# Attention rows of three query blocks turned by the PE instead of a transposing DMA, with three more decode pieces in the lead-in

## The chip, the cores and the metric

The kernel runs on one core of one Trainium2 chip. The metric is the device time of one execution in microseconds (us); the times given for the kernel before are a median of three runs. The engines are PE (TensorE, matmuls), DVE (VectorE), ACT (ScalarE), POOL (GpSimd) and SP (SyncE, which here only issues DMAs). Each engine works through its own instructions in order and waits at semaphores for the others.

## What is computed

Attention with a local window and a few global keys, then a dense layer pair, then a mixture of experts. Cut to what matters:

```python
# attention: batch 4, 8 heads, 768 positions, head size 64
scores = (q @ k.T) / 8 - slope[head] * dist        # masked: local window of 96 or 8 global keys
a = softmax(scores)
x = (a @ v) -> rows of 3072 tokens x 512
# dense layers: 512 -> 2048 -> 512
h = x @ w_in
g = where(h > 0, h, exp(min(h, 0)) - 1)
y = g @ w_out
# experts: 8 experts, each 512 -> 1024 -> 512, for tokens with y @ w_skip > 0
e = argmax(y @ w_gate); out = y + p[e] * (relu(y @ w1[e]) @ w2[e])
```

[...]

## The kernel before

The 3072 tokens are 24 query blocks of 128; three blocks make one group m of 384 tokens (`TB = 3`, `TN = 384`), and there are eight groups. Each block takes four attention steps (two heads each), so step t works on block t // 4. One step computes scores s (L239), adds bias and finds the maximum on DVE (L248), takes exps on ACT (L253), turns the probabilities (L293 on the PE in fp32 for the first blocks, L301 by a transposing DMA later) and, four steps behind, multiplies with the values into pv (L324). At a block's last step `att_pv` scales pv to the rows x (L338), and splits them in a high and a low f16 half, xs (L341 on ACT, L342 on DVE). `att_xturn` then turns xs, 128 x 1024 in f16, by one DMA_TRANSPOSE from SP's queue into xT (L348), the operand of the dense layers. It is called in the steps that follow.

A weight f of the dense layers (16 of them, each a slice of `w_in` and of `w_out`) is loaded as 1 MB of raw words (`w_load`, L396, into one of two staging buffers) and decoded in two halves (`w_prep`): part 0 is three integer operations of 1024 columns on DVE (L407, L408, L409), part 1 two casts on ACT (L415) and two subtractions on DVE (L416). `W_STEPS` says after which of the lead-in steps one such half is made. The load of weight f + 2 is asked for when part 0 of weight f has read its staging buffer.

The lead-in is the first 16 steps (blocks 0 to 3). There `keep_warm` puts 8 filler matmuls of 256 columns (40 in the first step) ahead of most steps (L354), to hold the PE's clock up. Then come the dense layers of group 0: for each f, h (L439, 12 matmuls of 384 columns, needs xT of three blocks), its nonlinearity on ACT and DVE (e: L443, L444, L446; gs: L449 and on POOL L450), and two f later y (L460, 9 matmuls of 512 columns). The attention of the next group and the rest of the decode run between. h has two PSUM buffers, so h of f + 2 waits until e of f has read the first.

The code is written in this program order; a scheduler then sets the order of each engine's instructions, except for those that `pin` holds. So an edit at one place shifts what stands next to what at others.

Of the kernel before, what the change touches and what calls it, by code (L numbers as in the profile page):

```python
# [10 lines left out]
F16 = DT.float16  # L11
I32 = DT.int32
U32 = DT.uint32
AF = mybir.ActivationFunctionType
# [5 lines left out]
P = 128  # L20
# [5 lines left out]
TB = 3  # L26
# [3 lines left out]
ND = DM // P  # L30
# [20 lines left out]

LP, LV = 1, 4

W_STEPS = (1, 2, 3, 4, 5, 6, 7, 8, 9, 10, 11, 12)
A_STEPS = ((0, 2, 4, 4, 6, 6, 7, 8, 10, 10, 12, 13),
           (0, 0, 1, 3, 6, 6, 7, 8, 11, 11, 12, 13))
EX_HALVES = (2, 2, 2, 2, 2, 2, 2, 2, 2, 2, 2, 3, 1, 2, 2, 2)
# [5 lines left out]
class Fast:  # L63
# [12 lines left out]
    def ct(self, shape, dt, name):  # L76
        return self.cp.tile(shape, dt, tag=name, name=name)


    def consts(self):  # L80
        nc, ct = self.nc, self.ct
        self.ident = ct([P, P], F32, "ident")
        make_identity(nc, self.ident)
        self.iota8 = ct([P, E], F32, "iota8")
        nc.gpsimd.iota(self.iota8, [[1, E]], base=0, channel_multiplier=0,
                       allow_small_or_imprecise_dtypes=True)
        self.tokid = ct([P, NTILE], F32, "tokid")
        nc.gpsimd.iota(self.tokid, [[P, NTILE]], base=0, channel_multiplier=1,
                       allow_small_or_imprecise_dtypes=True)
        self.tri = ct([P, 2, P], F16, "tri")  # L90
        nc.gpsimd.memset(self.tri, 1.0)
        nc.gpsimd.affine_select(out=self.tri[:, 0, :], in_=self.tri[:, 0, :], pattern=[[1, P]],
                                compare_op=ALU.is_gt, fill=0.0, base=0, channel_multiplier=-1)
        self.carry = ct([P, E], F32, "carry")
        nc.gpsimd.memset(self.carry, 0.0)
# [208 lines left out]
    def att_pv(self, g, xT, col):  # L304
        nc, ap = self.nc, self.ap
        n, hp = divmod(g, H // 2)
        i = n % NB
        if hp == 0:
            self.pvt[n] = self.ps.tile([P, H, D], F32, tag="pv", name=f"pv_{n}", bufs=1)
        pv, pT = self.pvt[n], self.pT.pop(g)  # L310
        nch = 2 if i else 1
        for j in range(2):
            h = self.heads(g)[j]
            mm = []
            if n < NPV:
                for c in range(nch):
                    v = self.vf[n] if c == nch - 1 else self.vf[n - 1]
                    mm.append((pT[:, j * nch + c, :], v[:, h, :]))
            for s_, x in ((0, 0), (0, 1), (1, 0)) if n >= NPV else ():
                for c in range(nch):  # L320
                    v = self.vv[n] if c == nch - 1 else self.vv[n - 1]
                    mm.append((pT[:, (j * 2 + s_) * nch + c, :], v[:, h, x, :]))
            for m, (l, r) in enumerate(mm):
                nc.tensor.matmul(pv[:, h, :], l, r, start=(m == 0), stop=(m == len(mm) - 1))  # L324
        if hp < H // 2 - 1:
            return
        if i + 1 < NB:
            if n >= NPV or self.both(n):
                nc.sync.dma_start(self.vv[n][PADK:PADK + 8], self.vg)
            else:  # L330
                nc.sync.dma_start(self.vf[n][PADK:PADK + 8],
                                  self.a["vp"][n - i, 0:8, :].rearrange("p (h d) -> p h d", h=H))
        st = self.st.pop(n)
        rs = ap.tile([P, H], F32, tag="rs", name=f"rs_{n}", bufs=2)
        nc.vector.tensor_scalar(rs, st[:, 1, :], 1e-9, 1.0 / VS if n < NPV else 1.0, ALU.add, ALU.mult)
        nc.vector.reciprocal(rs, rs)
        x = ap.tile([P, H, D], F32, tag="x", name=f"x_{n}", bufs=1)
        nc.vector.tensor_tensor_reduce(x, self.pvt.pop(n), rs.unsqueeze(2).to_broadcast([P, H, D]), 1.0, 0.0,  # L338
                                       ALU.mult, ALU.add, self.sq[:, 3, n:n + 1])
        xs = ap.tile([P, 2, H, D], F16, tag="xs", name=f"xs_{n}", bufs=1)  # L340
        nc.scalar.activation(xs[:, 0], x, AF.Copy)  # L341
        nc.vector.tensor_tensor(xs[:, 1], x, xs[:, 0], ALU.subtract)  # L342
        self.xs.append((xT[:, :, col:col + P], xs))

    def att_xturn(self):
        if self.xs:
            xT, xs = self.xs.pop(0)
            self.nc.sync.dma_start_transpose(xT, xs.rearrange("p s h d -> p (s h d)"))  # L348

    def keep_warm(self, t, n):  # L350
# [473 lines left out]
    def program(self, ep, wp, ap):  # L824
# [18 lines left out]
        def whalf():  # L843
            if done[0] < 2 * NF:
                f, part = divmod(done[0], 2)
                self.w_prep(f, part)
                done[0] += 1
                if part == 0 and f + 2 < NF:
                    self.w_load(f + 2)

        t = 0
        while t < 4 * TB + LV:
            self.att_step(t)
            if t == 2:
                self.att_split(0, 3)
                self.maxsq(self.vf0[:, 0, :], self.sq[:, 2, 0:1])
            for _ in range(W_STEPS.count(t)):
                whalf()
# [329 lines left out]
```

## Time and profile before

| | |
|---|---|
| median of three runs | 864.54 us (863.58 to 864.58) |
| the profiled execution | 866.19 us, its span 864.5 us |
| PE busy | 817.8 us, 95% of the span |
| DVE busy | 571.4 us, 66% |
| ACT busy | 530.0 us, 61% |
| POOL busy | 174.5 us, 20% |
| transposing DMAs xT<-xs | 24 |

Times in the trace are counted from the start of the span. [...] A DMA share is the mean busy share of the core's 16 DMA engines. In the rows further below, a bracket at a row's end is the time that the engine sat idle ahead of it and what ended that; busy times of neighbouring instructions on one engine overlap a little, so the step from one start to the next is the better price of one.

### The profile page before, as it was taken

The page shows a single profiled execution, that of the slowest core. Times are in us where ns is not written, and L with a number is a line of the kernel's source. Part 1 is how long each engine was busy: PE and PEld are TensorE (multiplying, and loading weights), DVE is VectorE, ACT ScalarE, POOL GpSimd, SP SyncE. Part 2 cuts the span into 40 slices and gives each one's busy share as a digit, 9 for nine tenths or more (in the row PEclk, how much of TensorE's full clock was granted, in tenths as well). Part 3 has the DMA queues.
Part 4 walks back from the last instruction along what each step waited for, and adds up shares of the span by engine and source line. Part 5 has one row for each costly group of instructions (what it writes and reads, how often), then busy time and mean ns, then how long its engine had stood idle before and what let it go on. Part 6 is the DMA issues. An engine that isn't in the chain of part 4 may idle for free.

```text
span 864.5 us, 17637 instructions
## 1 busy us (share of the span) xinstructions
PE 817.8 (95%) x6233; PEld 479.4 (55%) x6233; DVE 571.4 (66%) x1951; ACT 530.0 (61%) x1310; POOL 174.5 (20%) x201
## 2 busy tenths in 40 slices
PE   6997989999999999999999999999998869999995
PEld 4773445555555555555555555555555637666663
DVE  6997997575467567556666765644666846878622
ACT  4775767777767677767776776645655425555311
POOL 1001112123222322321322232232231010101110
PEclk9997999999999999999999999999999988999998
DMA  7999973644686487688659656321646779779510
GB/s 293 256 298 253 245 217 91 132 111 102 201 205 162 137 214 142 175 191 189 152 139 229 154 124 146 77 51 43 189 154 159 228 225 211 247 242 275 157 44 26
DMA packets 185394, 148.80 MB, mean 172 GB/s; under 512 B 152208, under 2 KB 154256, under 8 KB 181200
## 3 DMA queue, kind: packets, MB, share of 16 engines
q1 hardware_dynamic: 182096, 141.59, 63.0%
q0 software_dynamic: 3200, 5.99, 1.9%
q8 instruction: 51, 0.84, 0.4%
q14 instruction: 47, 0.39, 0.2%
HBM read 94.82 MB, written 21.08 MB: 134 GB/s over the span
## 4 chain that ended last, share of the span: by engine, by line
PE 72%; DVE 11%; DMA 10%; issue 4%; POOL 1%; ACT 1%; SPq 0%; POOLq 0%; DVEq 0%; ACTq 0%
PE h L439 25%; PE y L460 24%; PE eh L660 7%; PE eo L676 6%; PE s L239 5%; PE pv L324 4%; DMA eyT<-eyh 3%; DMA xg<-yt,pos 2%; DMA yg<-xg 2%; DVE ew L624 2%; DVE wt L408 2%; DVE wt L409 1%; PE warm L354 1%; DMA xT<-xs 1%; DVE w L416 1%
## 5 line engine op out<-in xcount | busy, mean ns | idle before, releaser
L439 PE MATMUL h<-xT,w 128*128 128x384 f16 x1536 | 274.9, 329 | 4.1 <-DMA xT<-xs 4.1
L460 PE MATMUL y<-w,gs 128*128 128x512 f16 x1152 | 271.4, 381 | 0.0
L439 PEld LDWEIGHTS <-w 128*128 128x128 f16 x1536 | 146.8, 99 | 106.4 <-issue 9.7
L450 POOL TENSOR_TENSOR gs<-e,gs 128x384 f16<-128x384 f32 x128 | 126.1, 987 | 393.9 <-ACT gs L449 329.2
L460 PEld LDWEIGHTS <-gs 128*128 128x128 f16 x1152 | 110.8, 98 | 119.9 <-issue 2.7
L446 DVE SCALAR_TENSOR_TENSOR e<-e,h 128x384 f32<-128x384 f32 x128 | 70.4, 551 | 99.6 <-ACT e L444 94.1
L449 ACT ACTIVATE gs<-e 128x384 f16<-128x384 f32 x128 | 66.7, 522 | 86.1 <-DVE e L446 84.9
L253 ACT ACTIVATE p<-p,st 128x232 f32<-128x232 f32 (+1 forms) x192 | 89.2, 465 | 38.4 <-DVE st L248 37.7
L660 PE MATMUL eh<-eyT,ew 128*128 128x128 f16 (+1 forms) x1152 | 103.6, 243 | 7.6 <-DMA eyT<-eyh 5.6
L676 PE MATMUL eo<-ew,ehs 128*128 128x512 f16 x384 | 102.0, 388 | 8.1 <-DVE ehs L664 8.1
L660 PEld LDWEIGHTS <-ew 128*128 128x128 f16 x1152 | 88.7, 101 | 32.8 <-issue 6.7
L624 DVE SCALAR_TENSOR_TENSOR ew<-er,ew 128x512 f16<-128x512 f32 x128 | 90.5, 725 | 15.9 <-ACT ew L623 14.5
L443 ACT ACTIVATE e<-h 128x384 f32<-128x384 f32 x128 | 61.6, 481 | 58.5 <-PE h L439 54.5
L662 ACT ACTIVATE ehs<-eh 128x128 f16<-128x128 f32 (+1 forms) x96 | 29.9, 311 | 102.3 <-PE eh L660 99.8
L248 DVE CUSTOM_DVE_ANT_0 p<-s,tab 128x232 f32<-128x232 f32 (+1 forms) x192 | 67.1, 377 | 20.3 <-PE s L239 18.6
L623 ACT ACTIVATE ew<-er 128x512 f16<-128x512 f32 x128 | 75.4, 620 | 4.5 <-DMA er<-in_moe_w 4.2
L283 DVE TENSOR_TENSOR ph<-p,ph 128x464 f16<-128x464 f32 x68 | 43.1, 648 | 40.2 <-ACT ph L282 40.2
L444 ACT ACTIVATE e<-e 128x384 f32<-128x384 f32 x128 | 66.6, 520 | 2.5
L664 DVE SCALAR_TENSOR_TENSOR ehs<-eh,ehs 128x128 f16<-128x128 f32 (+1 forms) x96 | 31.9, 332 | 36.9 <-ACT ehs L662 36.7
L676 PEld LDWEIGHTS <-ehs 128*128 128x128 f16 x384 | 35.4, 99 | 36.7 <-DVE ehs L664 12.7
L687 POOL DMA_INDIRECT out<-eres,ix x16 | 16.9, 1053 | 161.9 <-DVE eres L684 117.7
L239 PE MATMUL s<-qh 64*128 64x232 f16 (+1 forms) x432 | 40.0, 254 | 3.1 <-DVE st L248 2.5
(171 smaller groups left out, 849.4 us busy)
## 6 DMA issues: line engine op xcount, KB each, us to landing
er<-in_moe_w SPq DMA_DIRECT2D x64, 512.0 KB
wr<-in_wf SPq DMA_DIRECT2D x16, 1024.0 KB
wc<-in_wf SPq DMA_DIRECT2D x16, 1024.0 KB
qk<-in_qk SPq DMA_DIRECT2D x20, 720.0 KB
out<-yt SPq DMA_DIRECT2D x24, 256.0 KB
rawv<-in_vp SPq DMA_DIRECT2D x21, 256.0 KB
xg<-zrow SPq DMA_DIRECT2D x16, 257.0 KB
yg<-xg SPq DMA_DIRECT2D x16, 257.0 KB
```

What stands on the lines that cost most here:

```text
L239: nc.tensor.matmul(sp[j], q[r, hp, KW:], k[r, hp, KW - w:KW], start=(x == 0), stop=(x == len(mm) - 1))
L248: nc.vector.tensor_tensor_reduce(pw[:, j, :], sp[j], self.tab[:, h, :] if i else self.tab0[:, h, :], -0.125, 3e38, ALU.add, ALU.min, st[:, ...
L253: nc.scalar.activation(pw[:, j, :], pw[:, j, :], AF.Exp, bias=st[:, 0, h:h + 1], scale=-1.0, accum_out=st[:, 1, h:h + 1])
L439: nc.tensor.matmul(hps, wi[:, s_, c, :], xT[:, x * ND + c, :], start=(n == 0), stop=(n == 3 * ND - 1))
L446: nc.vector.scalar_tensor_tensor(g, e, -HS, hps, ALU.mult, ALU.max, accum_out=self.gsum[:, m * NF + f:m * NF + f + 1])
L449: nc.scalar.activation(gs[:, 0], g, AF.Copy)
L450: nc.gpsimd.tensor_tensor(gs[:, 1], g, gs[:, 0], ALU.subtract)
L460: nc.tensor.matmul(self.ys[m][t], gs[:, s_, t * P:(t + 1) * P], wo[:, x, :], start=(f == 0 and n == 0), stop=(f == NF - 1 and n == 2))
L623: self.pin(nc.scalar.activation(w[:, 0], r, AF.Copy, scale=sc))
L624: nc.vector.scalar_tensor_tensor(w[:, 1], r, sc, w[:, 0], ALU.mult, ALU.subtract, accum_out=self.esums[:, c:c + 1])
L660: nc.tensor.matmul(hps, l, r, start=(i == 0), stop=(i == len(mm) - 1))
L676: nc.tensor.matmul(self.eo[(e, t)], hs[:, s_, j * P:(j + 1) * P], self.ew[(e, 4 + f // 2, f % 2)][:, x, :], start=(f == 0 and n == 0), sto ...
```

## The change

`att_xturn` now turns the rows of blocks 0, 1 and 2 on the PE: eight transposes of 128 x 128 in f16, by an identity in f16 (`ident16`, cast once by DVE), into one PSUM tile of the tag `acc`, which ACT then copies to xT in one operation of 128 x 1024. The other 21 blocks keep the transposing DMA. And `W_STEPS` gets three more entries, so that 15 instead of 12 halves of decode are written into the lead-in's steps.

```diff
-W_STEPS = (1, 2, 3, 4, 5, 6, 7, 8, 9, 10, 11, 12)
+W_STEPS = (1, 2, 3, 4, 5, 6, 7, 8, 9, 10, 11, 12, 13, 14, 15)
...
         make_identity(nc, self.ident)
+        self.ident16 = self.ap.tile([P, P], F16, tag="ident16", name="ident16", bufs=1)
+        nc.vector.tensor_copy(self.ident16, self.ident)
...
-        self.xs.append((xT[:, :, col:col + P], xs))
+        self.xs.append((n, xT[:, :, col:col + P], xs))
 
     def att_xturn(self):
         if self.xs:
-            xT, xs = self.xs.pop(0)
+            n, xT, xs = self.xs.pop(0)
+            if n < TB:
+
+                tp = self.ps.tile([P, 2 * ND, P], F16, tag="acc", name=f"xtp_{n}", bufs=3)
+                for c in range(2 * ND):
+                    self.nc.tensor.transpose(tp[:, c, :], xs.rearrange("p s h d -> p (s h d)")[:, c * P:(c + 1) * P],
+                                             self.ident16)
+                self.nc.scalar.activation(xT, tp, AF.Copy)
+                return
             self.nc.sync.dma_start_transpose(xT, xs.rearrange("p s h d -> p (s h d)"))
```

The new lines move line numbers: L348 becomes L358, L407 to L409 become L417 to L419, L416 becomes L426, L439 becomes L449, L446 becomes L456. Numbers at the end of a name are buffers.

DVE, before: the end of the third block's rows (x_2, xs_2 are block 2; s0_16 and s1_16 the scores of step 16; wt_6, wr_6 weight 6, decoded and raw).

```order
L338 ISA x_2_773,sq_81<-pv_2_660,rs_2_770 128x512
L338 ISA sq_81 128x1
L248 ISA p_16_792,st_4_787<-s0_16_788,tab_146 128x232
L248 ISA st_4_787 128x1
L248 ISA p_16_792,st_4_787<-s1_16_789,tab_146 128x232
L248 ISA st_4_787 128x1
L409 SCALAR_TENSOR_TENSOR wt_6_831<-wr_6_555,wt_6_831 128x1024
L342 TENSOR_TENSOR xs_2_775<-x_2_773,xs_2_775 128x512
L407 TENSOR_SCALAR wt_7_863<-wr_7_638 128x1024
```

DVE, in the change: the same place.

```order
L250 ISA st_3_660 128x1
L337 TENSOR_SCALAR rs_2_802<-st_2_486 128x8
L417 TENSOR_SCALAR wt_7_819<-wr_7_649 128x1024
L338 RECIPROCAL rs_2_802<-rs_2_802 128x8
L418 SCALAR_TENSOR_TENSOR wt_7_819<-wr_7_649,wt_7_819 128x1024
L340 ISA x_2_805,sq_81<-pv_2_671,rs_2_802 128x512
L340 ISA sq_81 128x1
L419 SCALAR_TENSOR_TENSOR wt_7_819<-wr_7_649,wt_7_819 128x1024
L344 TENSOR_TENSOR xs_2_807<-x_2_805,xs_2_807 128x512
```

Weight 6 is through by then and the three integer operations of weight 7 stand ahead of xs_2; the scores of step 16 are read behind it.

DVE, before: up to the first operation on weight 9.

```order
L416 SCALAR_TENSOR_TENSOR w7_0_869<-wt_7_863,w7_0_869 128x512
L416 SCALAR_TENSOR_TENSOR w7_1_872<-wt_7_863,w7_1_872 128x512
L212 SCALAR_TENSOR_TENSOR vv_5_890<-rawv_5_714,vv_5_890 128x8x64
L407 TENSOR_SCALAR wt_8_919<-wr_8_835 128x1024
L248 ISA p_18_988,st_4_787<-s0_18_984,tab_146 128x232
L248 ISA st_4_787 128x1
L408 SCALAR_TENSOR_TENSOR wt_8_919<-wr_8_835,wt_8_919 128x1024
L248 ISA p_18_988,st_4_787<-s1_18_985,tab_146 128x232
L248 ISA st_4_787 128x1
L446 SCALAR_TENSOR_TENSOR e_0_0_824,gsum_122<-e_0_0_824,h_0_0_811 128x384
L409 SCALAR_TENSOR_TENSOR wt_8_919<-wr_8_835,wt_8_919 128x1024
L407 TENSOR_SCALAR wt_9_963<-wr_9_867 128x1024
```

DVE, in the change: from xs_2 (the row ahead of these) to the first operation on weight 9.

```order
L250 ISA p_16_830,st_4_825<-s0_16_826,tab_148 128x232
L250 ISA st_4_825 128x1
L250 ISA p_16_830,st_4_825<-s1_16_827,tab_148 128x232
L250 ISA st_4_825 128x1
L417 TENSOR_SCALAR wt_8_884<-wr_8_740 128x1024
L426 SCALAR_TENSOR_TENSOR w7_0_878<-wt_7_819,w7_0_878 128x512
L418 SCALAR_TENSOR_TENSOR wt_8_884<-wr_8_740,wt_8_884 128x1024
L250 ISA p_17_926,st_4_825<-s0_17_922,tab_148 128x232
L250 ISA st_4_825 128x1
L426 SCALAR_TENSOR_TENSOR w7_1_881<-wt_7_819,w7_1_881 128x512
L419 SCALAR_TENSOR_TENSOR wt_8_884<-wr_8_740,wt_8_884 128x1024
L417 TENSOR_SCALAR wt_9_916<-wr_9_823 128x1024
```

Weight 9 is taken up before the first e (e_0_0, the dense layer's f = 0) instead of behind it, and less stands between the decode of weight 7 and that of weight 9.

PE, before: the last rows ahead of the first h.

```order
L324 MATMUL pv_3_798<-vf_2_240,pTf_15_809 128x64
L324 MATMUL pv_3_798<-rawv_3_388,pTf_15_809 128x64
L324 MATMUL pv_3_798<-vf_2_240,pTf_15_809 128x64
L324 MATMUL pv_3_798<-rawv_3_388,pTf_15_809 128x64
L239 MATMUL s1_18_985<-qk_4_547 128x232
L439 LDWEIGHTS w0_0_275
L439 MATMUL h_0_0_811<-xT_0_343,w0_0_275 128x384
```

PE, in the change: the same place; eight transposes of xs_2, in three pieces between other work, end right ahead of these (a pv row of fp32 is two matmuls in the trace).

```order
L241 MATMUL s0_17_922<-qk_4_558 128x232
L241 MATMUL s1_17_923<-qk_4_558 128x232
L326 MATMUL pv_3_836<-vf_2_242,pTf_14_817 128x64
L326 MATMUL pv_3_836<-rawv_3_390,pTf_14_817 128x64
L326 MATMUL pv_3_836<-vf_2_242,pTf_14_817 128x64
L326 MATMUL pv_3_836<-rawv_3_390,pTf_14_817 128x64
L326 MATMUL pv_3_836<-vf_2_242,pTf_15_856 128x64
L326 MATMUL pv_3_836<-rawv_3_390,pTf_15_856 128x64
L326 MATMUL pv_3_836<-vf_2_242,pTf_15_856 128x64
L326 MATMUL pv_3_836<-rawv_3_390,pTf_15_856 128x64
L449 LDWEIGHTS w0_0_277
L449 MATMUL h_0_0_858<-xT_0_345,w0_0_277 128x384
```

The first h stands behind the scores of step 17 instead of step 18.

## Rows read from the trace of the kernel before

**Rows 1.** Busy time by stretch: us, PE, PEld, DVE, ACT, POOL (instructions), PEclk, DMA, GB/s
```profile
60.00:70.60 10.60, 4.78 (x33) 3.66 (x34) 9.10 (x19) 7.12 (x18) 0.00 (x0) 0.80 1.06 260
70.60:90.00 19.40, 19.40 (x89) 9.66 (x90) 14.80 (x29) 11.50 (x28) 5.02 (x4) 0.85 0.94 253
90.00:110.00 20.00, 17.86 (x118) 9.02 (x116) 18.60 (x40) 14.59 (x36) 3.14 (x3) 0.91 0.90 226
...
200.00:250.00 50.00, 49.92 (x380) 27.08 (x379) 28.78 (x89) 36.12 (x88) 12.64 (x14) 1.00 0.66 169
```

**Rows 2.** Chain of waits, 55 to 80 us: start us, us, what
```profile
61.01 9.41 DMA xT<-xs
```

**Rows 3.** Timeline of PE: start us, us, engine, line, operation, count [idle before, releaser]
```profile
47.03 1.04 PE L354 MATMUL warm<-tri 128*128 128x256 f16 x8
48.09 2.89 PE L324 MATMUL pv<-vf,pTf 128*128 128x64 f32 x24
...
65.75 0.66 PE L239 MATMUL s<-qk 64*128 64x232 f32 x2 [1.67 <-DVE st L248]
70.56 6.99 PE L439 MATMUL h<-xT,w 128*128 128x384 f16 x24 [4.15 <-DMA xT<-xs]
...
78.06 2.12 PE L439 MATMUL h<-xT,w 128*128 128x384 f16 x12
80.02 2.11 PE L460 MATMUL y<-w,gs 128*128 128x512 f16 x9
...
98.85 0.97 PE L239 MATMUL s<-qk 64*128 64x232 f32 x4 [2.14 <-DVE st L248]
...
120.17 0.86 PE L324 MATMUL pv<-vv,pT 128*128 128x64 f16 x24 [1.12 <-DVE sq L338]
...
149.19 0.47 PE L239 MATMUL s<-qh 64*128 64x232 f16 x6
```

**Rows 4.** Timeline of DVE, 55 to 126 us
```profile
55.13 0.69 DVE L212 SCALAR_TENSOR_TENSOR vv<-rawv,vv 128x512 f16<-128x512 f32 x1 [0.89 <-ACT vv L211]
...
59.16 1.22 DVE L409 SCALAR_TENSOR_TENSOR wt<-wr,wt 128x1024 int32<-128x1024 int32 x1
60.30 0.68 DVE L342 TENSOR_TENSOR xs<-x,xs 128x512 f16<-128x512 f32 x1
60.90 0.69 DVE L407 TENSOR_SCALAR wt<-wr 128x1024 int32<-128x1024 int32 x1
...
69.56 0.69 DVE L407 TENSOR_SCALAR wt<-wr 128x1024 int32<-128x1024 int32 x1 [1.50 <-DMA wr<-in_wf]
...
76.00 0.56 DVE L446 SCALAR_TENSOR_TENSOR e<-e,h 128x384 f32<-128x384 f32 x1 [3.98 <-ACT e L444]
...
105.32 0.40 DVE L248 CUSTOM_DVE_ANT_0 p<-s,tab 128x232 f32<-128x232 f32 x1 [1.34 <-PE s L239]
...
125.53 1.93 DVE L408 SCALAR_TENSOR_TENSOR wt<-wr,wt 128x1024 int32<-128x1024 int32 x1
```

**Rows 5.** Groups by line and shape, 30 to 60 us: busy us, mean ns, idle before
```profile
L253 ACT ACTIVATE p<-p,st 128x232 f32<-128x232 f32 x19 | 9.0, 478 | 1.2 <-DVE st L248 1.1
...
L172 ACT ACTIVATE junka<-qk 128x1024 f16<-128x1024 f32 x3 | 3.1, 1040 | 0.0
```

**Rows 6.** Busy time by stretch, finer (columns as in rows 1)
```profile
40.00:44.00 4.00, 3.64 (x26) 2.28 (x23) 4.00 (x9) 2.31 (x8) 0.14 (x1) 1.00 1.21 116
...
48.00:52.00 4.00, 3.98 (x34) 3.55 (x33) 3.98 (x12) 3.93 (x10) 0.00 (x0) 1.00 1.00 402
...
100.00:104.00 4.00, 4.00 (x14) 1.68 (x13) 3.98 (x11) 3.47 (x12) 0.00 (x0) 0.57 1.00 368
```

**Rows 7.** Timeline of the DMA queue of SyncE: issues of the first xT and of weight 8
```profile
36.16 1.63 SPq L348 DMA_TRANSPOSE xT<-xs  x1
...
60.41 0.33 SPq L396 DMA_DIRECT2D wr<-in_wf  x1
```

**Rows 8.** Chain of waits, 0 to 160 us: the load of weight 4
```profile
29.11 7.67 DMA wr<-in_wf
```

## The prediction

> **What bounds the kernel now.** I read the busy shares by stage first, then the chain of waits across the start of the feed-forward layers, then the two engines that meet there. The stage table [rows 1] shows the place: between 60 and 70.6 us the PE is busy for 4.78 of 10.6 us and its clock is granted at 0.80; until 110 us the granted clock stays below 1.00. The chain of waits names the cause [rows 2]: 9.41 us from the issue of the third transposing DMA, which turns the third block's attention rows (xs) into xT, until it lands. The PE's own rows agree [rows 3]: it waits 1.67 us for a score buffer, does 0.66 us of work and waits 4.15 us for xT; then the 24 matmuls of the first two h take 6.99 us, where two h and their y later go by in 1.96 us each. So 70.56 us is when h starts, and some 3.1 us more go to the half clock.
>
> A wait of the PE is worth only what the engine next in line lets through. That engine is DVE, which decodes the weights, reads the scores and makes the rows in one fixed order. Its idle rows [rows 4] are few: 0.89 us for ACT, 1.50 for a weight load, 3.98 for the first e (the PE was late), 1.34 for scores. By stage [rows 1] it is idle 1.50, 4.60 and 1.40 us in the three stretches between 60 and 110 us; with the 0.89 that is **8.39 us**. Later the PE is busy 49.92 of 50 us at a granted clock of 1.00 [rows 1], so what the first scores of block 28 gain, at 149.19 us [rows 3], the end gains too. I make the sum to that point.
>
> **The change part by part.**
>
> *The cast of the identity* is one DVE operation of 128x128, some 0.2 us, ahead of the tables; there DVE soon waits for its first weight load anyway. I count 0; if that cover is gone it costs 0.2.
>
> *The transposes.* The trace has no f16 transpose on the PE. The nearest row is the filler matmul: 8 of 256 columns in 1.04 us [rows 3], so 8 of 128 columns take about half, 0.5 to 0.6 us; above lie the fp32 matmuls of 64 columns, 24 in 2.89 us, which is 0.96 for eight. I take 0.6. For blocks 0 and 1 the PE waits for nothing new: xs stands on DVE ahead of the score reads that the next scores need anyway. Were it late, the fillers, scores and pv queued behind the transposes would wait with it. The rows show the clock at 1.00 from 48 to 52 us, where fp32 transposes, fillers and pv are mixed [rows 6]. [...] *The copies to xT* are 128x1024 on ACT; the row of that size took 1.04 us [rows 5]. ACT is busy 7.12 of 10.6 us in the stretch ahead of h [rows 1], so I count the first two at nothing; without that room each puts off the exps behind it by up to 1.04. The third is on the way to h, below.
>
> *The way to the first h.* Three more pieces mean that L407, L408, L409 of weight 7 and both L416 of weight 6 now stand ahead of the third xs, and two score reads no longer do. By start to start [rows 4] L409 (and L408) costs 1.14 us and a 512-column operation 0.60, L407 as much; a score read, 0.40 long, 0.32 by the same overlap. That is 2.88 + 1.20 - 0.64 = 3.44 us later; the 0.89 us for ACT falls away, since its place in the order now has decode behind it. So xs, done at 60.90 us, is done at 60.90 + 3.44 - 0.89 = 63.45. Behind it the PE waits for two score reads (0.64) and then does the next scores (0.66) and 16 pv matmuls of 64 columns (24 took 2.89 us: 1.93) [rows 3]: h at **66.7** us. ACT is ready before: a read 0.32, two exps of 0.48, the copy 1.04 [rows 5], at 65.8. So h starts 3.9 us sooner; bounds 3.0 (the 0.89 stays) and 4.8 (ACT alone decides).
>
> *What DVE then lets through.* Ahead of e of f=8 DVE's list now holds what it held ahead of L408 of the last weight at 125.53 us [rows 4], plus L408 and L409 (2.28) and the cast, less one block's x, xs and reciprocal, e of f=9 and two small reductions (1.95): 0.43 us more, so 125.96 us at the old pace. The PE's h of f=10 needs the buffer that this e frees. From there to the scores of block 28 stand, in the new order, six h and six y (1.955 each from 78.06 to 80.02 and on, 23.5), three scores (0.3 each) and pv of 24, 12 and 12 matmuls (0.86, 0.43, 0.43): **26.0** us [rows 3], the scores by the 0.47 of 232 columns, less for 128. If all 8.39 us of DVE's idle time go and none is new, block 28 starts at 125.96 - 8.39 + 26.0 = 143.57, against 149.19: 5.6 us sooner. The PE's side can pay that: 3.9 from the start and up to 3.1 from the clock.
>
> *New waits of DVE.* Decode runs further ahead, and its raw weights have two staging buffers: the load of weight 9 can start only when L409 of weight 7 is done. In the new order 5.64 us of DVE work stand between the two (0.60 + 0.64 + 0.60 + 0.60 + 1.14 + 0.32 + 0.60 + 1.14), for weight 11 it is 5.94. Two loads can be read whole: 7.67 us and, from issue at 60.41 to the end of DVE's wait at 69.56, 9.15 us [rows 8, 7, 4]. A load of 1 MB at the 260 GB/s of that stretch [rows 1] takes 4.0 us. Both were in a crowded queue. Behind the issue of the first xT at 36.16 us [rows 7], 116 GB/s moved at a share of 1.21 from 40 to 44 us, later 402 at 1.00 [rows 6], which is 2.8 us of traffic lost in four; three such transfers go from SP's queue, and the writes of zero rows move up into their places. [...] I put loads of about 6 us, so 0.8 us of waits in all, bounds 0 and 9.7 (below), and 0.5 for a hand-over like the 0.89 one. Sum: 5.6 - 1.3 = **4.3 us** gained. The profiled execution took 866.19 us, 1.65 over the median of 864.54; it would take 861.9, and the median **860.2**.
>
> **The rivals.**
>
> *Nothing new waits.* Loads land in time, the 0.5 doesn't come: 5.6 us, **858.9**; up to one more if fewer of DVE's operations run long, as that L408 did with 1.93 us where L409 took 1.22 [rows 4].
>
> *The clock still falls ahead of h.* In the new order the PE stands before the third block's transposes until xs has its first f16 half; an estimate of that gap is 2 us, since nothing else is queued ahead and L409 with xs alone take 1.74 [rows 4]. A gap of 2.14 us at 98.85 was followed by 0.57 granted [rows 3, 6]; behind one of 1.12 at 120.17, 24 matmuls passed in 0.86 [rows 3]. If it falls, the 16 pv matmuls (1.93) and the first h (1.96) take twice as long and DVE waits 3.8 us for e: 4.3 - 3.8 = 0.5 gained, **864.0**. [...]
>
> *Loads as slow as the first.* At 7.67 us weights 9 and 11 cost 2.03 + 1.73 = 3.8 us: 5.6 - 3.8 - 0.5 = 1.3 gained, **863.2**.
>
> *Slower.* Loads as slow as the 9.15: 3.5 + 3.2 at weights 9 and 11, and about 3.0 at the others, whose windows in the new order are 7.6 to 8.8 us; 9.7 in all. 5.6 - 9.7 = 4.1 lost, **868.6**. Against it stands that the transposing DMA beside that load is gone. It decides from about 8.5 us a load.
>
> *It doesn't do what it says.* Another wait holds h where it was (the score that sits ahead of it on the PE, or the loads): **864.5**.
>
> **How the numbers follow.** Forecast 0.50, nothing new waits 0.18, clock 0.11, slow loads 0.10, very slow loads 0.07, no effect 0.04. A measurement of this kernel tells about 0.2% (1.7 us) from no change. Faster by more: 0.50 + 0.18 and half of the clock and load cases that end near 863, 0.06, so 0.74; slower 0.07; the same 0.19. The range takes in the first two cases, the clock and the slow loads: 857.6 to 864.0.
>
> **What would show it.** Right: h begins near 66.7 us, its first two pass in about 4 us at a granted clock of 1.00, DVE has under 2 us of idle time from 60 to 110 us, and scores of block 28 start near 145 us. Eight f16 transposes take 0.6 us and the copy 1.0. Wrong: waits of L407 for its load above 1 us; a granted clock near 0.5 at 62 to 70 us; PE waits behind DVE that add up to more than before.

## The result, and the profile after

Before: 865.08 us median of 17 runs; after: **873.05 us** median of 17 (867.56 to 879.51). The ratio is 1.009 with a 95% interval of 1.0073 to 1.0107. The change makes the kernel slower by some 8 us. I had forecast 860.2 and a range of 857.6 to 864.0. The profiled execution of after has a span of 872.7 us.

The first view is busy time by stretch, in the columns of [rows 1]; the first three lines are its first three stretches, then two finer ones.

```profile
60.00:70.60 10.60, 7.49 (x37) 5.82 (x38) 8.67 (x21) 6.17 (x17) 0.00 (x0) 0.78 0.96 316
70.60:90.00 19.40, 19.40 (x90) 11.25 (x88) 13.56 (x24) 10.93 (x24) 4.15 (x3) 0.77 0.64 184
90.00:110.00 20.00, 16.46 (x115) 8.59 (x114) 20.00 (x39) 13.43 (x31) 3.47 (x3) 1.00 0.81 226
...
35.00:37.00 2.00, 2.00 (x14) 1.85 (x14) 2.00 (x7) 2.00 (x5) 0.00 (x0) 0.54 1.13 421
...
68.00:74.00 6.00, 6.00 (x31) 5.23 (x29) 4.33 (x7) 4.47 (x11) 0.00 (x0) 0.50 0.29 117
```

From 60 to 70.6 us the PE is now busy for 7.49 us where it was 4.78 [rows 1], yet it does not arrive sooner: the granted clock (the column PEclk, a share of TensorE's full speed) is 0.50 from 68 to 74 us while the PE is busy all the time, and 0.54 near 36 us. In the kernel before it was 1.00 there:

```profile
36.00:40.00 4.00, 4.00 (x36) 3.56 (x36) 3.95 (x13) 3.95 (x14) 0.14 (x1) 1.00 1.03 341
```

What the PE did in the changed kernel stands in its timeline of after (columns of [rows 3]).

```profile
34.19 1.98 PE L326 MATMUL pv<-vf,pTf 128*128 128x64 f32 x12 [0.56 <-DVE sq L340]
...
64.88 0.23 PE L354 MATMUL xtp<-ident,xs 128*128 128x128 f16 x1 [1.71 <-ACT xs L343]
65.89 0.66 PE L326 MATMUL pv<-vf,pTf 128*128 128x64 f32 x2 [0.79 <-DVE xs L344]
...
67.62 0.53 PE L354 MATMUL xtp<-ident,xs 128*128 128x128 f16 x3
...
69.65 0.63 PE L354 MATMUL xtp<-ident,xs 128*128 128x128 f16 x4
70.21 1.15 PE L241 MATMUL s<-qk 64*128 64x232 f32 x4
...
74.76 6.42 PE L449 MATMUL h<-xT,w 128*128 128x384 f16 x24
...
157.39 0.47 PE L241 MATMUL s<-qh 64*128 64x232 f16 x6
```

The wait of 4.15 us for xT [rows 3] is gone. In its place are two gaps, 1.71 and 0.79 us, in front of the third block's transposes and of the fourth block's pv. Behind them everything is at half clock: a pair of pv matmuls starts every 0.43 us (0.22 at a clock of 1.00, in the kernel before from 60 to 62 us), and from 65.89 to the first h pass 8.87 us. So h starts at 74.76 instead of 70.56, 4.2 us later, and its first 24 matmuls take 6.42 us, nearly what they took before (6.99). Block 28's first scores start at 157.39 instead of 149.19 [rows 3]: 8.2 us later, which is the loss at the end too (872.7 against 864.5 of span). Half of it is there at the first h, half arises between h and block 28. DVE's timeline of after, answering [rows 4]:

```profile
39.45 0.40 DVE L250 CUSTOM_DVE_ANT_0 p<-s,tab 128x232 f32<-128x232 f32 x1 [1.73 <-PE s L241]
...
63.47 0.68 DVE L340 CUSTOM_DVE_ANT_1 x<-pv,rs 128x512 f32<-128x512 f32 x1
...
65.21 0.68 DVE L344 TENSOR_TENSOR xs<-x,xs 128x512 f16<-128x512 f32 x1
...
69.08 0.69 DVE L426 SCALAR_TENSOR_TENSOR w<-wt,w 128x512 f16<-128x512 f32 x1 [1.93 <-ACT w L425]
...
79.88 0.69 DVE L426 SCALAR_TENSOR_TENSOR w<-wt,w 128x512 f16<-128x512 f32 x1 [5.24 <-ACT w L425]
```

DVE's idle time, which the change was to use up, is still there. It waits 1.73 us for scores that stand on the PE behind transposes and fillers at half clock (0.50 from 36 to 38 us), and 1.93 and 5.24 us for ACT, whose half of the decode stands in its order behind copies that wait for the PE (pTf behind pv, e behind h). Two lines give the sum, from 53 us to the start of the e of f=8, first of the kernel before, then of after.

```profile
53.00:118.13 65.13, 56.92 (x341) 31.50 (x338) 56.57 (x124) 43.60 (x109) 9.62 (x9) 0.90 0.96 252
```

```profile
53.00:129.18 76.18, 65.69 (x382) 38.50 (x383) 67.80 (x138) 49.64 (x121) 10.02 (x9) 0.91 0.76 220
```

Before, DVE was busy 56.57 of 65.13 us, 8.56 idle; after, 67.80 of 76.18, 8.38 idle. So 11 us more of DVE's work stand ahead of this e, and as the idle time did not shrink, the e comes 11 us later. The additional decode (of weights that come as 64-bit floats, taken as pairs of 32-bit words) is some 7.6 us of it: two each of L417, L418 and L419 and three L426 more than before, at the prices of the prediction. Most of the rest are operations that ran longer than their like. Five L417 took 1.40 us or more, where every L407 before took about 0.7; why is not shown. The first of them, in DVE's timeline of after:

```profile
88.59 1.40 DVE L417 TENSOR_SCALAR wt<-wr 128x1024 int32<-128x1024 int32 x1
```

### The profile page after: what moved, and what is told of

Read it like the earlier page. It is cut to its first block, busy times and chain, and to the rows that moved or that the text cites. A ratio compares the mean times of both kernels' runs of the same rounds, so it can differ in the third digit from the quotient of the medians.

```text
span 872.7 us, 17679 instructions
## 1 busy us (share of the span) xinstructions
PE 824.2 (94%) x6257; PEld 483.7 (55%) x6257; DVE 571.8 (66%) x1952; ACT 533.3 (61%) x1313; POOL 172.6 (20%) x201
## 4 chain that ended last, share of the span: by engine, by line
PE 72%; DVE 13%; DMA 8%; issue 4%; ACT 1%; POOL 1%; SPq 0%; POOLq 0%; DVEq 0%
PE h L449 24%; PE y L470 23%; PE eh L670 6%; PE eo L686 6%; PE pv L326 5%; PE s L241 5%; DMA eyT<-eyh 3%; DVE ew L634 2%; DMA xg<-yt,pos 2%; PE warm L364 2%; DVE w L426 1%; DVE wt L418 1%; DVE wt L419 1%; DMA yg<-xg 1%; DVE wt L417 1%
## 5 line engine op out<-in xcount | busy, mean ns | idle before, releaser
L449 PE MATMUL h<-xT,w 128*128 128x384 f16 x1536 | 274.7, 329 | 3.5 <-DVE e L456 3.5
L449 PEld LDWEIGHTS <-w 128*128 128x128 f16 x1536 | 147.1, 99 | 105.6 <-issue 9.2
L456 DVE SCALAR_TENSOR_TENSOR e<-e,h 128x384 f32<-128x384 f32 x128 | 70.4, 550 | 95.6 <-ACT e L454 88.3
L285 DVE TENSOR_TENSOR ph<-p,ph 128x464 f16<-128x464 f32 x68 | 45.3, 681 | 41.1 <-ACT ph L284 41.1
L326 PE MATMUL pv<-vv,pT 128*128 128x64 f16 x888 | 41.7, 195 | 1.9 <-DMA pT<-ph 1.9
```

Source lines behind the costliest of these rows:

```text
L449: nc.tensor.matmul(hps, wi[:, s_, c, :], xT[:, x * ND + c, :], start=(n == 0), stop=(n == 3 * ND - 1))
L456: nc.vector.scalar_tensor_tensor(g, e, -HS, hps, ALU.mult, ALU.max, accum_out=self.gsum[:, m * NF + f:m * NF + f + 1])
```

## The experiments

Two theories at first. **Clock**: the gaps of the PE drop its clock, and the half clock is the loss. **Decode**: the three pieces ahead of the third block's rows make everything late. Later, when the decode's place behind the first h was in question, the rival was called **order**: what counts is DVE's work ahead of the e of f=8.

| run | PE turns | pieces | other | us | ratio, 95% interval |
|---|---|---|---|---|---|
| e1 | all three | 12 | | 865.27 | 1.0000, 0.9981 to 1.0019 |
| e2 | none | 15 | | 865.05 | 1.0003, 0.9979 to 1.0027 |
| e3 | third | 15 | | 867.76 | 1.0037, 1.0019 to 1.0056 |
| e5 | third | 12 | | 863.14 | 0.9991, 0.9969 to 1.0014 |
| e10 | first two | 12 | | 868.76 | 1.0054, 1.0029 to 1.0079 |
| e4 | all three | 15 | fillers ahead of transposes | 867.41 | 1.0026, 1.0003 to 1.0049 |
| e9 | third | 15 | filler, early | 867.07 | 1.0016, 0.9996 to 1.0036 |
| e12 | third | 15 | fillers in the gap | 863.44 | 0.9985, 0.9967 to 1.0004 |
| e16 | all three | 15 | fillers in the last gap | 866.60 | 1.0021, 1.0000 to 1.0043 |
| e17 | all three | 15 | fillers in all three gaps | 865.30 | 1.0022, 0.9998 to 1.0045 |
| e6 | none | 12 | one or two pieces per h | 863.13 | 0.9988, 0.9965 to 1.0011 |
| e13 | none | 12 | one per h | 866.40 | 1.0020, 0.9997 to 1.0044 |
| e7 | all three | 15 | one or two per h | 870.84 | 1.0087, 1.0060 to 1.0114 |
| e14 | all three | 15 | one per h | 867.06 | 1.0017, 0.9992 to 1.0041 |
| e8 | third | 12 | one or two per h | 858.10 | 0.9923, 0.9901 to 0.9946 |
| e11 | third | 12 | one per h | 855.28 | 0.9904, 0.9881 to 0.9927 |
| e15 | third | 10 | one per h | 859.34 | 0.9929, 0.9902 to 0.9955 |

Ratios are to the kernel before, run beside each (its medians lay between 864.3 and 865.1). One execution of each version is traced, and it need not be a middle one: e3's took 870.35 us, the longest of its ten, e5's 858.97, e12's 860.80 and e17's 861.66, each the shortest of ten. From the first scores of block 28 to the end of the span the traces have 709.4 (e12) to 718.3 us (e8), 715.3 in both kernels. So what block 28 gains, the end gains only to within some 4 us: the traces below tell what happens up to block 28, the medians what a version is worth.

### Which part of the change

The transposes alone (e1), from the changed kernel:

```diff
-W_STEPS = (1, 2, 3, 4, 5, 6, 7, 8, 9, 10, 11, 12, 13, 14, 15)
+W_STEPS = (1, 2, 3, 4, 5, 6, 7, 8, 9, 10, 11, 12)
```

> The changed kernel with the twelve decode pieces of before in the lead-in; the PE transposes of all three blocks stay. Clock theory (the loss comes from two falls of the PE's clock, each behind a gap in front of the transposes, near 34 and near 63 us): both gaps are in this order too, since the transposes of the first block still stand ahead of the fillers, so the first fall (half clock from about 34 to 38 us) is seen again, the first h is at 70 us or later, and the time is 866 to 871 us. Decode theory (the three pieces put the third xs 3.4 us later and everything follows from that): without them xs comes near 61 us, h near 66 us, and the time is 861 us or less.

The pieces alone (e2) are the same line the other way round, in the kernel before.

> The kernel before with fifteen decode pieces in the lead-in; the rows are still turned by the transposing DMA. Clock theory: the fillers stand where they stood, no half clock near 34 us; the wait for xT moves with xs, about 2.5 to 3.4 us later, h near 73 to 74 us, but the decode work that DVE has done by then is not waited for later, so the time is 863 to 867 us. Decode theory: the three pieces are the loss, h is near 74 us as in the changed kernel and block 28 starts near 157 us: 870 us or more.

The third block alone, with fifteen pieces (e3), and with twelve (e5):

```diff
-            if n < TB:
+            if n == TB - 1:
```

> The changed kernel in which only the third block is turned by the PE, the first two by the transposing DMA as before; fifteen pieces. In its order twelve pv matmuls stand ahead of the third block's transposes, and the first fillers stand ahead of pv again. Clock theory: no fall near 34 us, xs about 63.5 us, h at 67 to 70 us; 860 to 864 us. Decode theory: as the changed kernel, 870 to 874 us.

> Only the third block turned by the PE, the first two by the transposing DMA, and the twelve decode pieces of before. Order theory (what sets the end is DVE's work ahead of the e of f=8, which three more pieces make longer by about 7 us, plus DVE's idle time before it): that work is as in the kernel before, so the time moves by the idle time alone; xs at 61 us, h at 67 to 68 us, 3 us less idle time: 861 to 863 us. Clock theory (the gap in front of the transposes drops the clock, and that is the loss): half clock for some 14 us from 62 us on, h no sooner than 70 us: 865 to 868 us.

Only the first two blocks (e10) is `n < TB - 1` with twelve pieces.

> Only the first two blocks turned by the PE, the third by the transposing DMA, twelve pieces. If moving pv and fillers around the transposes is what the first two cost: half clock near 35 us, the third xs at 63 to 64 us instead of 61, xT some 2 us later than before, 866 to 869 us. If the first two are free (their xT is not needed before 70 us): 864 to 865 us.

Neither the transposes nor the pieces alone move the time that can be measured; together they cost 8 us. Neither theory had e1 or e3 right: 865.27 us lie below the 866 to 871 of the clock theory and above the 861 of the decode theory, 867.76 between 860 to 864 and 870 to 874. The decode theory, as I had put it, falls with e2: the pieces are free where the transposing DMA stays, although the PE is at half pace there too: from 61.54 us on a pair of pv matmuls starts every 0.43 us. There xT lands soon after the PE is through with what stands in front (PE's timeline of e2):

```profile
71.53 6.38 PE L439 MATMUL h<-xT,w 128*128 128x384 f16 x24 [0.56 <-DMA xT<-xs]
```

e5 shows what the transposes are worth when nothing disturbs them. PE's timeline, then busy time by stretch:

```profile
60.88 0.40 PE L354 MATMUL xtp<-ident,xs 128*128 128x128 f16 x4
...
62.73 0.39 PE L354 MATMUL xtp<-ident,xs 128*128 128x128 f16 x4
...
64.53 4.07 PE L449 MATMUL h<-xT,w 128*128 128x384 f16 x24
...
146.34 0.47 PE L241 MATMUL s<-qh 64*128 64x232 f16 x6
```

```profile
60.00:70.00 10.00, 10.00 (x68) 6.43 (x67) 8.79 (x19) 9.13 (x23) 0.01 (x1) 1.00 0.95 317
...
110.00:130.00 20.00, 14.38 (x121) 7.49 (x120) 19.82 (x49) 14.05 (x34) 2.39 (x3) 0.97 0.66 168
```

The PE is busy throughout at a clock of 1.00, h starts 6.0 us sooner than before and its first two pass in 4.07 us. That was the aim of the change. Only 2.9 us of it are left at block 28 (146.34 for 149.19), since from 110 to 130 us DVE is full and the PE busy for 14.38 of 20 us. My rough 67 to 68 us for its h was too late, and the 861 to 863 us a little low; by its interval (0.9969 to 1.0014) the time is not clear of no change.

With three pieces more (e3) the gain turns into a loss. Its PE timeline, and its stretch from 53 us to the e of f=8:

```profile
62.74 0.69 PE L326 MATMUL pv<-vf,pTf 128*128 128x64 f32 x2 [1.05 <-DVE sq L340]
...
68.34 0.63 PE L354 MATMUL xtp<-ident,xs 128*128 128x128 f16 x4
...
71.74 5.81 PE L449 MATMUL h<-xT,w 128*128 128x384 f16 x24
```

```profile
53.00:129.00 76.00, 66.22 (x364) 37.40 (x364) 66.38 (x137) 47.63 (x116) 10.70 (x9) 0.87 0.88 228
```

The pieces stand on DVE ahead of x (L340) of the third block. The fourth block's pv has one buffer, which that x frees, so the PE waits 1.05 us for it, after 0.49 us of another gap. From there to h pass 9.0 us, at half clock (0.50 from 62 to 74 us).

For the first two blocks the gap comes from the PE's own order: before, the filler matmuls stood in front of pv and covered its wait for x [rows 3]; now the transposes have drawn pv in front of the fillers. e1 has it too, and one thing more. PE's timeline of e1:

```profile
34.41 1.82 PE L326 MATMUL pv<-vf,pTf 128*128 128x64 f32 x12 [0.58 <-DVE sq L340]
...
65.82 0.41 PE L326 MATMUL pv<-vf,pTf 128*128 128x64 f32 x2 [1.65 <-DMA vf<-in_vp]
...
70.08 5.53 PE L449 MATMUL h<-xT,w 128*128 128x384 f16 x24
```

The third block's pv matmuls are spread behind transposes and fillers, so the small load that patches eight rows into vf once they are done goes out late (issued at 61.71 us here, at 60.76 in the changed kernel, at 52.81 in the kernel before, by the timelines of SyncE's queue), and the fourth block's pv waits 1.65 us for it. In e10 these shifts stand alone: xs of the third block at 68.9 us, h at 77.2 us, 868.76 us. The half clock that I had expected near 35 us did not come (seven fillers pass in 0.93 us from 36.94 us on, in 1.70 at 36.40 in the changed kernel); it came from 52 to 58 and from 72 to 76 us, at 0.50.

### How much of it is the clock

> The changed kernel with eight filler matmuls (1 us at full clock) issued ahead of each block's transposes. Clock theory: the gaps near 34 and 63 us are covered, the granted clock stays at or near 1.00 until h, h is at 67 to 69 us; 860 to 865 us. Decode theory: no gain, the fillers add up to 3 us of PE work ahead of h: 873 us or more.

```diff
+                self.keep_warm(100 + n, 8)
                 tp = self.ps.tile([P, 2 * ND, P], F16, tag="acc", name=f"xtp_{n}", bufs=3)
```

> The third block turned by the PE with fifteen pieces, and eight more filler matmuls ahead of the scores of step 16, where the PE had 1.5 us of gaps before the pv of the fourth block; the order of the engines is otherwise that of the run without them. Clock theory (the late x costs 1.5 us of waiting, and the half clock behind the gap costs as much again or more): the clock stays at 1.00, the 9.0 us from the first of these pv to h become 4.5 to 5, h at 67 to 68 us instead of 71.7, and some 3 to 4 us of the 4.6 that the three pieces cost come back: 863 to 865 us. If the three pieces cost their time through DVE's order alone: h sooner, yet 867 to 868 us.

```diff
-        if t < 4 * TB + LV:
+        if t < 4 * TB + LV + 1:
             self.keep_warm(t, 8 if t else 40)
```

Both were blunt, and both missed the times of the clock theory. In e4 the fillers changed the order once more (the third xs at 70.5 us, h at 74.45 with its first two in 4.06 us). In e9 they came to stand 2 us ahead of the gap, a wait of 0.89 us for x was left, the clock fell all the same (0.76 from 62 to 64 us, 0.50 from 64 to 72) and h was at 69.6 us. That h is sooner and the time 867.07 us is what I had written for the pieces costing by DVE's order alone, but with the clock down the run tells the two no better apart. The clean form puts fillers into the gap itself and leaves DVE's order as it is (up to 140 us the traces show the same): e12 for the third block alone, e16 and e17 for the changed kernel.

```diff
+            if t == 4 * TB + LV:
+                self.keep_warm(t, 14)
             self.att_pv(g, self.xT[m], c * P)
```

> The run of the third block alone with fifteen pieces, with fourteen filler matmuls (1.8 us at full clock) exactly in the PE's gaps ahead of the pv of the fourth block; every engine's order is otherwise the same. Clock theory: the fillers cover the 1.5 us of gaps, the clock stays at 1.00, h at 67 to 68.5 us instead of 71.7, first two h in about 4 us instead of 5.8, time 862 to 865 us. If the clock is not what the gap costs: h within 1 us of 71.7, 867 to 869 us.

```diff
+            if t in (8, 12, 16):
+                self.keep_warm(t, 20 if t == 16 else 8)
             self.att_pv(g, self.xT[m], c * P)
```

> The changed kernel, its order unchanged, with twenty filler matmuls (2.6 us at full clock) in the PE's gaps ahead of the third block's transposes and the pv behind them (1.71 and 0.79 us). Clock theory: the clock stays at 1.00 there, the 8.9 us from the first of these pv to h become about 4.5, h at 70 to 71 us instead of 74.8, DVE's idle time ahead of the e of f=8 falls by 4 us or more, 866 to 869 us. If the late x and the order are the loss and not the clock: h within 1.5 us of 74.8, 871 to 874 us.

> As the run before it, with eight fillers (1 us) as well in the gap in front of the pv of the second and the third block (0.56 and 0.89 us). Clock theory: the half clock of 3.4 us near 35 us goes too and with it 1.7 us of DVE's idle time; the third xs at 64 us instead of 65.9, h at 68 to 69.5 us, 863 to 867 us. If the first two blocks' transposes cost by their place in the order and not by the clock: no better than the run with the third gap alone.

(e16 has only the line for t of 16.) PE's timeline of e12, then two fine stretches and the one to the e of f=8:

```profile
60.71 3.12 PE L364 MATMUL warm<-tri 128*128 128x256 f16 x14
...
63.89 0.33 PE L326 MATMUL pv<-vf,pTf 128*128 128x64 f32 x2
...
65.18 0.39 PE L354 MATMUL xtp<-ident,xs 128*128 128x128 f16 x4
65.40 0.39 PE L326 MATMUL pv<-vf,pTf 128*128 128x64 f32 x2
...
68.59 4.06 PE L451 MATMUL h<-xT,w 128*128 128x384 f16 x24
```

```profile
62.00:64.00 2.00, 2.00 (x13) 1.54 (x11) 2.00 (x5) 1.65 (x3) 0.00 (x0) 0.59 1.07 395
64.00:66.00 2.00, 2.00 (x23) 2.00 (x21) 0.92 (x3) 1.01 (x2) 0.00 (x0) 1.00 1.13 268
...
53.00:121.80 68.80, 60.70 (x371) 33.75 (x371) 65.59 (x133) 46.81 (x115) 10.70 (x9) 0.95 0.90 245
```

The clock did not stay at 1.00, as I had expected: it is 0.56 from 60 to 62 and 0.59 from 62 to 64 us, and 14 fillers take 3.12 us where 8 had taken 1.04. But now the half clock passes over fillers, and from 64 us on it is 1.00, when pv, transposes and h come. (The wait of 1.05 us is filled here and the clock fell all the same, so that wait is not what brings it down; which gap does is open.) Against e3 the fillers let pv start 1.15 us later (63.89 for 62.74), and yet h starts 3.15 us sooner: pv, transposes and scores take 4.7 us instead of 9.0. (e3's execution was 0.7 us late already at the second block's xs; that is no part of the effect, and leaves 2.4 us.) DVE's idle time falls from 9.62 to 3.21 us, and the time from 867.76 to 863.44. That is the price of the three pieces: e5 without them took 863.14. So what they cost was the clock, not their place in DVE's order, within the intervals of some 2 us. In e16 and e17 the clock held (1.00 from 60 to 110 us), and they are the cleanest reading of the case. PE's timelines of e16 and of e17:

```profile
64.15 2.36 PE L364 MATMUL warm<-tri 128*128 128x256 f16 x20
...
71.32 4.06 PE L451 MATMUL h<-xT,w 128*128 128x384 f16 x24
```

```profile
63.20 2.36 PE L364 MATMUL warm<-tri 128*128 128x256 f16 x20
...
65.67 0.39 PE L326 MATMUL pv<-vf,pTf 128*128 128x64 f32 x2
...
70.37 4.06 PE L451 MATMUL h<-xT,w 128*128 128x384 f16 x24
...
149.88 0.47 PE L241 MATMUL s<-qh 64*128 64x232 f16 x6
```

In the changed kernel 20 fillers in the last gap (e16) bring 873.05 down to 866.60, 6.4 us (6.0 by the ratios). The granted clock is 1.00 up to h and beyond, and although xs is done 1.4 us later than in the changed kernel, h starts 3.4 us sooner. Fillers in all three gaps give 865.30, no different from e16 (1.0022 and 1.0021). Block 28 starts in e17 at 149.88 us, 0.7 us behind the kernel before. So most of the 8.2 us at block 28 is the half clock ahead of h: 6.5 come back in e16, where block 28 starts at 150.88 us. That the half clock near 35 us costs anything is not shown: e17 is rid of it (1.00 from 33 to 39 us), yet its third xs is done at 66.37 us and h at 70.37, where I had expected 64 and 68 to 69.5, since pv of the third block now waits 1.39 us for the patch of vf and DVE behind it. Against the order of e5, what is left is h at 70.37 us instead of 64.53: the pieces ahead of x, the order of the PE and the late patch, which no run tells apart.

### The order of the decode behind the first h

```diff
             if m == 0:
-                for _ in range(2):
+                for _ in range(1 + f % 2):
                     whalf()
```

> The kernel before with the decode of the first group spread: after h of f, one piece where f is even and two where it is odd, instead of two each time. DVE's work ahead of the e of f=8 holds 26 pieces for 28, ahead of the e of f=10 28 for 32. Order theory: h of f=10 to 14 start sooner by 2 to 5 us, 860 to 863 us. Clock theory: nothing ahead of 80 us changes, 864 to 866 us.

> The changed kernel with the same spread: 27.5 pieces instead of 31 ahead of the e of f=8, some 7 us of DVE work less. Nothing ahead of the first h changes. Order theory: the 4 us that are lost between the first h and block 28 come back, h still near 75 us: 866 to 869 us. Clock theory: 871 to 874 us.

> Only the third block turned by the PE, twelve pieces, and the spread of the decode. Order theory: both gains add, 24 pieces ahead of the e of f=8: 856 to 861 us. Clock theory: as the third block alone with twelve pieces, 865 to 868 us.

With `range(1)`, and in e15 with ten entries in W_STEPS:

> The third block by the PE, twelve pieces, and one decode piece after each h of the first group (and those that the next h needs). Ahead of the e of f=8 stand 23.5 pieces for 24 in the run with one or two, ahead of the e of f=10 26 for 27.5. Order theory: within 2 us of that run, 856 to 860 us. If the gain there came from something else: back to 863 us.

> The kernel before, with the transposing DMAs, and one decode piece after each h of the first group instead of two. DVE's work ahead of the e of f=8 and f=10 is 94.7 and 103.7 us against 94.9 and 108.3. Order theory: block 28 comes 2 to 5 us sooner, 859 to 863 us. If the order of the decode only helps where the PE turns the third block: 864 to 866 us.

> The changed kernel, its transposes and fifteen pieces as they are, and one decode piece after each h of the first group instead of two. The way to the first h is unchanged (h near 75 us). Order theory: of the 8 us the part that arises behind the first h, some 4 us, comes back: 867 to 870 us. If the late first h decides alone: 872 to 874 us.

> The third block by the PE, ten pieces in the lead-in instead of twelve, and one after each h of the first group. Ahead of the e of f=8 DVE has 87.8 us of work instead of 90.3. Order theory: up to 2.5 us faster than the run with twelve, 852 to 856 us, as long as no h waits for its weight; if the twelve are needed because later h wait for decode: 856 to 860 us.

Where h starts early, DVE is what the PE waits for, and decode that is not needed yet stands in front of each e. Spreading it then pays, within what I had expected for e8 and a little more for e11: 863.14 becomes 858.10 (e8) and 855.28 us (e11), the fastest version here, faster than the kernel before by 1%. Busy time of e11 from 110 to 130 us:

```profile
110.00:130.00 20.00, 18.21 (x155) 10.14 (x154) 19.99 (x49) 13.12 (x36) 4.97 (x5) 1.00 0.75 223
```

The PE is busy for 18.21 us there, 14.38 in e5, and block 28 starts at 139.26 us. Where h starts late, the order theory did badly. In the kernel before one or two pieces per h (e6, 863.13 us) can't be told from no change, and one per h gives nothing (e13, I had expected 859 to 863 us): DVE's idle time up to the e of f=8 is still 8.48 us, and the clock is at 0.53 from 96 to 103 us, where it was 0.82. e7 missed its 866 to 869 us, though its h of f=15 starts 3.0 us sooner than in the changed kernel; e14 met its range. Ten pieces (e15) are no better than twelve: 859.34 us, where the order theory had 852 to 856. Why e14 gives back 6 us and e7 only 2 stays open. At the h of f=15 their traces had gained 4.6 and 3.0 us, but e7's traced execution (867.81 us) is the shortest of its six and e14's (870.19) one of its longer ones, so these traces can't decide it.

## Why the prediction was wrong

The step that failed is the way from xs to the first h, taken at full clock, and with it the idle time of DVE that h was to use up. The forecast had 3.25 us for that way and h at 66.7 us; measured are 8.87 us at a granted clock of 0.50 and h at 74.76 us. Of 8.39 us of idle time all was to go and 1.3 to come; 8.38 us are there. The clock is shown as the cause by e16, where fillers alone, with the order kept, bring 6.4 us back.

**The costs of the parts held.** The cast moved nothing: L419 near 28 us starts 0.25 us sooner than L409 did. Transposes and copy have these rows in the changed kernel (columns of [rows 5], 30 to 75 us):

```profile
L354 PE MATMUL xtp<-ident,xs 128*128 128x128 f16 x24 | 3.4, 279 | 1.7 <-ACT xs L343 1.7
...
L356 ACT ACTIVATE xT<-xtp 128x1024 f16<-128x1024 f16 x3 | 3.1, 1017 | 1.1 <-PE xtp L354 1.1
```

The 279 ns are from start to end, most of them at half clock (220 in e5, at a clock of 1.00); but in e12 four start within 0.22 us (the pv behind them at 65.40, they at 65.18), so eight take 0.45 us, against my 0.6. The copy takes 1.02 us, I had 1.04. The loads, whose very slow case was my only way to a loss, cost nothing: from 30 to 160 us DVE never waits for one; I had 0.8.

**"For blocks 0 and 1 the PE waits for nothing new" was wrong.** I looked at who makes xs and not at what left its place. The fillers that had covered pv's wait for x stood behind the transposes now. A gap of 0.56 us at 33.6 us, half clock behind it, DVE 1.73 us late: with 0.53 us for ACT that I had taken to fall away, xs was done at 65.89 us instead of 63.45. (In e17, without that half clock, other waits make xs as late; the gap and the shifted order are shown, the clock's part in this one is not.) The sum of 3.44 less 0.89 us for the three pieces was itself right: from the second block's xs to the third's pass 13.6 us in e12 and 11.2 in e5.

**The way from xs to h was undersized.** I had 3.25 us, for the reads, scores and 16 pv matmuls behind the last transposes. At full clock it is 4.00 (e17, from 66.37 to 70.37), for part of the 16 pv matmuls among the transposes had been waiting too. At the clock granted it was 8.87. So of the 8.1 us by which h missed my 66.7, 2.4 are the late xs, 0.8 the pv that I left out and 4.9 the clock.

**The clock was a rival with a chance of 0.11, and it is what happened.** I had written down the gap, an estimate of 2 us, and set it aside because a gap of 1.12 us elsewhere had been followed by full speed [rows 3] (1.00 from 120 to 122 us). Its price, 3.8 us, was too small: I doubled 16 pv matmuls and one h, but all 32 pv matmuls and the transposes and scores among them ran at half clock, then the first h and the start of the second (6.42 us for the two, 4.06 in e16), and DVE's idle time followed, 6.4 us in all (e16). So even its time, 864.0, was too low, and the whole range lay below the measured one.

**"All 8.39 us of DVE's idle time go" carried the sum**, and it comes near to holding only with the clock at 1.00: 2.31 us are left from 53 us on in e17, 8.38 in the changed kernel. Even in e17 block 28 starts at 149.88, not at 145: DVE stands idle 2.89 us from 10 to 53 us, where it was 1.28 in the kernel before, 1.0 us more than forecast from 53 us on, and the remaining 2.4 us are longer operations of DVE and the PE's way behind the e of f=8 (27.2 us, I had 26.0). So even with the clock held up the forecast is too good by 5 us: e17 took 865.30 us, not 860.2, and no gain of the change is measured.

**That the transposes themselves bring the clock down is not shown.** The clock fell behind gaps (1.71 and 0.79 us in the changed kernel), and in e5 and e17 the same transposes pass among other matmuls at a granted clock of 1.00 (60 to 64 us, 64 to 68 us). No run here has transposes alone for long enough to show more.

## What to carry to other kernels

When a wait is taken away, look at what the waiting engine does in the microseconds before its new place: a filler that has moved by one position can open a gap of half a microsecond (0.56 us here), and a clock that falls behind such gaps can cost more than the wait did (here 6 to 8 us, for a wait of 4.15). Before judging a change by its time, put filler work exactly into the new gap with the order kept; here that told the clock (6 to 8 us) from the order (what is left in e17, a ratio of 1.0022, is not clear of no change) with one line. Read the clock in the filled gap too: in e12 the fillers took the half clock upon themselves (0.56 and 0.59 over them), in e16 it was 1.00 over them. And work done ahead of need is free only while its engine would otherwise idle: with h early, decoding later, not sooner, was worth 5 to 8 us.

## What the runs showed of the hardware

The length of a gap does not tell alone whether the clock falls. In the changed kernel 0.56 us at 33.6 us were followed by 0.54 granted, 0.89 us at 49.1 by 1.00; in e16 a gap of 0.57 us in the same place (pv at 35.32) by 1.00. Behind a wait of 1.26 us ahead of the third block's pv seven fillers take 1.70 us in e16, and behind one of 1.39 us in the same place 0.93 us in e17 (they took 1.70 in the changed kernel with 0.50 granted from 36 to 38 us, 0.93 with 1.00 from 51 to 53). PE's timelines of after, of e16 and of e17, then busy time by stretch of e16 and of after:

```profile
50.03 1.55 PE L326 MATMUL pv<-vf,pTf 128*128 128x64 f32 x12 [0.89 <-DVE sq L340]
```

```profile
35.32 1.55 PE L326 MATMUL pv<-vf,pTf 128*128 128x64 f32 x12 [0.57 <-DVE sq L340]
...
49.88 1.72 PE L326 MATMUL pv<-vf,pTf 128*128 128x64 f32 x12 [1.26 <-DMA vf<-in_vp]
...
51.81 1.70 PE L364 MATMUL warm<-tri 128*128 128x256 f16 x7
```

```profile
50.53 1.52 PE L326 MATMUL pv<-vf,pTf 128*128 128x64 f32 x12 [1.39 <-DMA vf<-in_vp]
...
52.11 0.93 PE L364 MATMUL warm<-tri 128*128 128x256 f16 x7
```

```profile
35.00:37.00 2.00, 1.68 (x17) 1.68 (x18) 2.00 (x5) 1.70 (x4) 0.04 (x1) 1.00 0.99 396
```

```profile
51.00:53.00 2.00, 2.00 (x24) 1.76 (x24) 2.00 (x8) 2.00 (x6) 0.00 (x0) 1.00 0.77 137
```

What else decides is not shown. In the changed kernel the clock, once down, stayed down under full load: the PE was busy in every microsecond from 66 to 78, at 0.50 throughout. The transposing DMA, for all its 9.41 us [rows 2], was no worse for the whole than this: with it and fifteen pieces (e2) the time is that of the kernel before.
